# The opening of a gated-GLU and spectral kernel: weights on a second queue, pinned orders, and the left-over columns split after the transpose

## The chip, the cores and the metric

One core of a Trainium2 chip runs the whole program. The metric is device time in microseconds of one execution; three executions of the kernel before took 1441.42, 1441.58 and 1442.97 us (median 1441.58). A separate execution was profiled; its trace gives the rows below. Its span, from the first to the last instruction, is 1439.6 us.

The engines: TensorE (PE in the profile; PEld is its weight load), VectorE (DVE), ScalarE (ACT), GpSimd (POOL) and SyncE (SP), which here only issues transfers. ScalarE can issue transfers too, on a queue of its own.

## The reference

With S = 2048 rows, D = 576 columns, F = 4608 hidden columns, all in float32:

```python
xn = layernorm(x)                                   # over the 576 columns, eps 1e-5
X  = rfft2(xn) * (w_r + 1j * w_i)                   # over rows and columns
A  = irfft2(X, s=(2048, 576))
B  = (sigmoid(xn @ w_gate) * (xn @ w_up)) @ w_down
return x + A + B
```

## The kernel before

**Numbers.** A float32 matrix is split into a high part (rounded to fp32r, which TensorE takes at full rate) and a low part (the rest). A product is the sum of high x high, low x high and high x low.

**Rows.** The 2048 rows go in two halves ("pairs", p = 0 and 1) of eight tiles of 128 rows; a half is two chunks (c = 0, 1) of four tiles (m = 0 to 3), 512 rows each. The 576 columns of x are two blocks of 288 = 128 + 128 + 32. The 32 left-over columns get one matmul of 96 rows: high, high and low part stacked against high, low and high part of the weights. So a product of a 288-block with a 128-column weight block is seven matmuls of 128x512: four for the high and low combinations of `STEPS` on the 256 columns with high x, two with low x, one for the stacked left-over columns (index 2 in X and in w).

**Blocks of weights.** F is 36 blocks (f, or u = f + 36p) of 128 columns. `load_raw` brings a block's gate and up columns into `raw` (four quarters: B12, B22, B21, B11; two pieces per quarter, the second one copying the 32 left-over rows four times), eight transfers per block, two buffers. The first two blocks (`make_p`, f = 0, 1) use the four quarters as they are (`plain`: four products of a chunk); the later ones (`make_w`, `unit`) form sums of quarters for seven products in place of eight. `parts` rounds on ScalarE (L231) and makes the low parts on VectorE (L233, and L235 for 32 rows of the stacked piece). The result is stored to memory (`wsp`) for the second half, where `get_w` loads it instead.

**The transposed input.** X holds seven 288-blocks of the normalised rows, transposed, in fp32r: A11, A12 (chunk 0), A21, A22 (chunk 1), and the sums S1 to S4. `moments` and `scales` give mean and 1/std (VectorE, with a ScalarE square root in the opening, L360); `prep_hi` normalises a tile (ScalarE, L409). `fill(p, k, mm)` makes two tiles of one block: six transposes on TensorE into a PSUM pair (L438, L439), two copies on ScalarE (L442 high parts; L443 the left-over columns), one subtraction on VectorE (L444, low parts). The left-over columns are split before the transpose: `rem_hi` (ScalarE, L391) writes two copies of the high part, `rem_lo` (VectorE, L396) the low part, for two blocks at once, and TensorE transposes the 96 columns (L439). There are 16 fills in a half, four of them in the opening.

**Order.** A scheduler places instructions by program order and by when it takes their inputs to be ready; `placed` (through `keep_in_program_order`) pins one behind what stands before it on its engine, while `late_input` is set. Each engine and each queue then runs strictly in order.

**The opening.** L889: x tiles 0 to 3 on SP, raw block 0, tiles 4 and 5, raw block 1, tiles 6 and 7. TensorE multiplies by an identity meanwhile (L904, L922). Tiles 0 and 1 are normalised, then 2 and 3; A11 and A12 are filled for tiles 0, 1 and then 2, 3; block 0 is split (`mk`); the statistics of tiles 4 to 7 follow (L931). `plain` then runs (f, c) = (0,0), (1,0), (0,1), (1,1) in the banks A or B and E; beside it chunk 1 is prepared (`second_chunk`), then S1 to S4 (`factors`, `late`), and blocks 2 and 3 are made. From `unit` 2 on, the down products (`down`, `po`) run between the products, and VectorE adds them to `acc`.

**PSUM.** Two pairs of banks (tag pp) are shared by the fills, the down products and the later stages; single banks A, B, and two E.

Of the kernel before, what the change touches and what calls it, by code (L numbers as in the profile page):

```python
# [16 lines left out]
P = 128  # L17
# [115 lines left out]
def spectral_glu_kernel(ctx: ExitStack, tc: tile.TileContext, x, w_r, w_i, w_gate, w_up, w_down, out):  # L133
# [77 lines left out]
    def load_raw(f):  # L211
        cols = slice(f * P, (f + 1) * P)

        RAW[f] = raw = R["pool"].tile([P, 4, 3, P], F32, tag="raw", name=f"raw{f}", bufs=2)
        for src, blks in ((w_gate, (3, 2)), (w_up, (0, 1))):
            v = src.rearrange("(h r) f -> h r f", h=2)
            for h, b in enumerate(blks):
                nc.sync.dma_start(raw[:, b, :KT, :], v[h, :KT * P, cols].rearrange("(k p) f -> p k f", p=P))  # L218
                nc.sync.dma_start(raw[:, b, KT, :], v[h:h + 1, KT * P:, cols].to_broadcast([4, REM, P]))
# [8 lines left out]
    def parts(w, src, i, n):  # L228

        o = w[:, i:i + n]  # L230
        placed(nc.scalar.activation(o[:, :, :3, :], src, AF.Copy))  # L231
        yield
        placed(nc.vector.tensor_tensor(o[:, :, 3:, :], src[:, :, :KT, :], f32(o[:, :, :KT, :]), op=OP.subtract))  # L233
        r = slice(REM, 2 * REM)
        nc.vector.tensor_tensor(o[r, :, KT, :], src[r, :, KT, :], f32(o[r, :, KT, :]), op=OP.subtract)  # L235
        yield
# [28 lines left out]
    def make_p(f):  # L265
# [76 lines left out]
    def stats(srcs, t0, pool, table=False):  # L342

        for k, src in enumerate(srcs):
            moments(src, t0 + k, pool)
        scales(t0, len(srcs), pool, table)

# [6 lines left out]
    def scales(t0, n, pool, table):  # L354
# [3 lines left out]
        nc.vector.tensor_scalar(ve, mv[:, ts, 1], EPS, None, op0=OP.add)  # L358
        if table:
            nc.scalar.activation(w0, ve, AF.Sqrt)  # L360
            nc.vector.reciprocal(r0, w0)
            steps = 1
        else:

            nc.vector.tensor_scalar(w1.bitcast(I32), ve.bitcast(I32), 1, None, op0=OP.logical_shift_right)
            nc.vector.tensor_scalar(r0.bitcast(I32), w1.bitcast(I32), -1.0, float(0x5F3759DF), op0=OP.mult, op1=OP.add)
            steps = 3
        nc.vector.tensor_scalar(ve, ve, -0.5, None, op0=OP.mult)
# [14 lines left out]
    XS, XR, RM = {}, {}, {}  # L383
# [4 lines left out]
    def rem_hi(p, m, i, tag, bufs):  # L388
        rem = XS[m][:, i:i + 2, KT * P:]
        rm = R["pool"].tile([P, 2, 3, REM], F32R, tag=tag, name=f"{tag}{p}_{m}_{i}", bufs=bufs)  # L390
        nc.scalar.activation(rm[:, :, :2], rem.unsqueeze(2).to_broadcast([P, 2, 2, REM]), AF.Copy)  # L391
        RM[m, i] = rm

    def rem_lo(m, i):
        rm = RM[m, i]
        placed(nc.vector.tensor_tensor(rm[:, :, 2], XS[m][:, i:i + 2, KT * P:], f32(rm[:, :, 0]), op=OP.subtract))  # L396
        for k in range(2):
            XR[m, i + k] = rm[:, k].rearrange("p a b -> p (a b)")

    def rem_parts(p, m, i, tag, bufs):  # L400
        rem_hi(p, m, i, tag, bufs)
        rem_lo(m, i)

    def prep_hi(p, m, c):
# [5 lines left out]
        rem_hi(p, m, 2 * c, "rma", 2)  # L410

    def prep_lo(m, c):
        rem_lo(m, 2 * c)

    def prep(p, m, c):
        prep_hi(p, m, c)
        prep_lo(m, c)

    def sums(p, m):
# [5 lines left out]
        rem_parts(p, m, 3, "rma", 2)  # L425
        rem_parts(p, m, 1, "rm34", TPC)

    XP = {"A11": 0, "A12": 1, "A21": 2, "A22": 3, "S4": 1, "S3": 2, "S2": 3, "S1": 4}

    def fill(p, k, mm):  # L430

        i, j0 = XA[k], XP[k]
        cols = slice(2 * mm * P, (2 * mm + 2) * P)
        pt = pair(f"px{p}_{k}_{mm}")
        for j in range(2):
            m = 2 * mm + j
            for q in range(KT):
                nc.tensor.transpose(pt[:, 0, (2 * q + j) * P:(2 * q + j + 1) * P], XS[m][:, j0, q * P:(q + 1) * P], idf)  # L438
            nc.tensor.transpose(pt[:KR, 1, j * P:(j + 1) * P].bitcast(F32R), XR[m, j0], idr)  # L439
        v = pt[:, 0].rearrange("p (q s) -> p q s", q=KT)  # L440
        o = X[:, i, :, cols]
        nc.scalar.activation(o[:, :KT], v, AF.Copy)  # L442
        nc.scalar.activation(o[:KR, KT], pt[:KR, 1, :2 * P], AF.Copy)  # L443
        nc.vector.tensor_tensor(o[:, KT + 1:], v, f32(o[:, :KT]), op=OP.subtract)  # L444
# [201 lines left out]
    def prod(bank, w, x, start, stop, skip=False):  # L646
        for j, (sx, sw) in enumerate(STEPS):
            nc.tensor.matmul(bank, w[:, sw, :], X[:, x, sx, :], start=start and j == 0, stop=stop and j == len(STEPS) - 1,  # L648
# [11 lines left out]
    def plain(u, c, beside):  # L660
# [7 lines left out]
        for i, (b, k) in enumerate(((0, 1), (0, 2), (1, 1), (1, 2))):  # L668
            prod(bank[b], w[:, WP[f"B{k}{b + 1}"]], XA[f"A{c + 1}{k}"], k == 1, k == 2)
# [215 lines left out]
    nc.vector.memset(rstd[:, :1], 1.0)  # L885
    nc.scalar.dma_start(f32(idr), con["id"])
    nc.scalar.dma_start(idf, con["id"])
    nc.scalar.activation(nmr[:, :1], rstd[:, :1], AF.Sqrt)
# [14 lines left out]
    for n, (o, r) in enumerate(todo):  # L903
        nc.tensor.matmul(o, idr[r], eye[r], start=id(o) not in opened, stop=n + 2 >= len(todo), skip_group_check=True)  # L904
        opened.add(id(o))
    for m in range(TPC):
        new_xs(0, m)
    mk = make_p(0)
    for m in (0, 1):
        moments(acc[m], m, R["pool"])  # L910
    scales(0, 2, R["pool"], True)
    for m in (0, 1):
        prep_hi(0, m, 0)
    for m in (2, 3):
        moments(acc[m], m, R["pool"])
    for m in (0, 1):
        prep_lo(m, 0)
    scales(2, 2, R["pool"], True)
    for k in ("A11", "A12"):
        fill(0, k, 0)  # L920
# [225 lines left out]
```

## Time and profile before

| | |
|---|---|
| median of three runs | 1441.58 us (1441.42 to 1442.97) |
| the profiled execution | span 1439.6 us |
| TensorE matmul busy | 1425.9 us, 99% |
| VectorE busy | 1093.5 us, 76% |
| ScalarE busy | 652.3 us, 45% |
| GpSimd busy | 4.8 us |
| mean granted TensorE clock | 0.996 |

How the rows are read. A timeline row gives start (us from the span's start), time taken, engine, line, operation, out<-in tiles, shape and count; in brackets the idle time of that engine just before it and what ended it. A row of waits gives engine, tile and line, whom it waited for, then total us, times, longest. A row of a stretch gives its bounds and length, then busy us and number of instructions of PE, PEld, DVE, ACT and POOL, the granted TensorE clock (1.00 is full), the share of DMA time and GB/s. A row of a line or tile gives operation, tiles, count, shortest/median/longest ns, first and last start. A row of the chain gives start, length and what the end of the program was waiting for at that time. SPq and ACTq are transfers being issued.

### The profile page before, as it was taken

How to read it: one execution, taken by the hardware profiler on the slowest of the kernel's cores; microseconds unless marked ns; L12 is line 12 of the kernel's file. 1: busy time of each engine (PE TensorE's matmuls, PEld its weight loads, DVE VectorE, ACT ScalarE, POOL GpSimd, SP SyncE). 2: the span in 40 equal slices, each digit the busy share in tenths (PEclk: the TensorE clock that was granted, in tenths of full speed). 3: DMA queues.
4: the chain of work that ended last, by engine and by line, in shares of the span. 5: the costliest groups of instructions: out<-in, count | busy, mean ns of one | idle time of the engine just before them, and what ended most of it. 6: DMA issues, size and time to landing. Idle time of an engine off the chain costs nothing.

```text
span 1439.6 us, 21954 instructions
## 1 busy us (share of the span) xinstructions
PE 1425.9 (99%) x8073; PEld 1254.3 (87%) x8073; DVE 1093.5 (76%) x1798; ACT 652.3 (45%) x1122; POOL 4.8 (0%) x21
## 2 busy tenths in 40 slices
PE   8999999999999999999999999999999999999998
PEld 5888888888888888888888888888888889899997
DVE  6988788888888888756366787767888877766784
ACT  5644444444444444444345444444555534443432
POOL 0000000000000000000000000000000000000000
PEclk8999999999999999999999999999999999999999
DMA  6588788787777778664667767668998887776642
GB/s 209 207 277 294 263 295 285 254 274 258 263 261 255 262 254 277 230 231 167 226 210 203 212 197 214 196 198 275 271 275 272 267 276 246 228 224 198 204 126 83
DMA packets 184747, 338.86 MB, mean 235 GB/s; under 512 B 15808, under 2 KB 108480, under 8 KB 179776
## 3 DMA queue, kind: packets, MB, share of 16 engines
q1 hardware_dynamic: 183712, 336.15, 72.2%
q8 instruction: 64, 1.05, 0.3%
q10 hardware_dynamic: 928, 1.31, 0.3%
q14 instruction: 43, 0.35, 0.1%
HBM read 201.28 MB, written 136.12 MB: 234 GB/s over the span
## 4 chain that ended last, share of the span: by engine, by line
PE 94%; DVE 2%; DMA 1%; SPq 1%; ACT 1%; issue 1%; DVEq 0%; ACTq 0%
PE pB L648 23%; PE po L755 18%; PE pE L648 16%; PE pA L648 15%; PE ps L846 12%; PE pd L491 2%; PE pe L605 2%; PE pc L549 1%; PE py L576 1%; PE pa L503 1%; PE pb L532 1%; DMA raw<-in_B_w_up 1%; PE pf L475 1%; PE pz L588 1%; SPq L218 0%
## 5 line engine op out<-in xcount | busy, mean ns | idle before, releaser
L648 PE MATMUL pB<-X,w 128*128 128x512 f32 x1484 | 383.0, 395 | 1.9 <-ACT w L231 1.5
L648 PEld LDWEIGHTS pB<-X,w 128*128 128x128 f32 x1484 | 267.8, 188 | 51.8 <-ACT w L231 1.9
L648 PE MATMUL pE<-X,w 128*128 128x512 f32 x1064 | 272.5, 392 | 0.2 <-DVE y L713 0.2
L648 PE MATMUL pA<-X,w 128*128 128x512 f32 x1008 | 259.4, 395 | 0.3 <-DVE X L444 0.2
L648 PEld LDWEIGHTS pE<-X,w 128*128 128x128 f32 x1064 | 192.7, 188 | 34.6 <-DVE y L713 0.7
L648 PEld LDWEIGHTS pA<-X,w 128*128 128x128 f32 x1008 | 184.5, 190 | 33.9 <-DVE X L444 0.7
L755 PE MATMUL po<-wd,hh 128*128 128x288 f32 x1216 | 210.9, 295 | 0.0
L846 PE MATMUL ps<-wf,hs 128*128 128x288 f32 x1260 | 206.0, 296 | 0.3 <-issue 0.3
L846 PEld LDWEIGHTS ps<-wf,hs 128*128 128x128 f32 x1260 | 189.3, 188 | 19.4 <-DVE qs L856 1.9
L755 PEld LDWEIGHTS po<-wd,hh 128*128 128x128 f32 x1216 | 184.4, 188 | 11.2
L759 DVE TENSOR_TENSOR acc<-acc,po 128x576 f32<-128x576 f32 x168 | 126.0, 750 | 77.9 <-PE po L755 76.8
L231 ACT ACTIVATE w<-raw 128x768 fp32r<-128x768 f32 (+1 forms) x106 | 100.8, 952 | 115.6 <-PE pE L648 47.5
L755 PE MATMUL po<-wd,hl 128*128 128x288 f32 x608 | 128.9, 293 | 0.0
L856 DVE TENSOR_TENSOR qs<-qs,ps 128x576 f32<-128x576 f32 x112 | 84.1, 751 | 28.6 <-PE ps L846 27.9
L755 PEld LDWEIGHTS po<-wd,hl 128*128 128x128 f32 x608 | 98.7, 189 | 0.0
L733 DVE TENSOR_TENSOR y<-y,g 128x1024 f32<-128x1024 f32 x67 | 82.0, 1223 | 4.4 <-DVE y L732 0.5
L233 DVE TENSOR_TENSOR w<-raw,w 128x512 fp32r<-128x512 f32 (+1 forms) x106 | 82.0, 773 | 4.3 <-ACT w L231 3.3
L856 DVE TENSOR_TENSOR acc<-acc,ps 128x576 f32<-128x576 f32 x90 | 67.5, 750 | 22.9 <-PE ps L846 22.5
L716 ACT ACTIVATE g<-pB 128x512 f32<-128x512 f32 x68 | 40.7, 598 | 93.6 <-PE pB L648 93.5
L782 ACT ACTIVATE hs<-y 128x512 fp32r<-128x512 f32 x105 | 64.5, 628 | 34.3 <-DVE y L820 10.3
L732 DVE TENSOR_TENSOR y<-v,pE 128x512 f32<-128x512 f32 x67 | 45.9, 686 | 39.4 <-PE pE L648 39.3
L713 DVE TENSOR_TENSOR y<-v,pE 128x512 f32<-128x512 f32 x68 | 46.7, 687 | 33.7 <-ACT v L712 33.0
(166 smaller groups left out, 1678.8 us busy)
## 6 DMA issues: line engine op xcount, KB each, us to landing
w<-wsp SPq DMA_DIRECT2D x246, 320.0 KB
wsp<-w SPq DMA_DIRECT2D x34, 2240.0 KB
wdsp<-wd SPq DMA_DIRECT2D x36, 576.0 KB
wf<-tsp SPq DMA_DIRECT2D x60, 288.0 KB
wf<-wdsp SPq DMA_DIRECT2D x45, 288.0 KB
std<-in_B_w_down SPq DMA_DIRECT2D x36, 288.0 KB
raw<-in_B_w_gate SPq DMA_DIRECT2D x72, 128.0 KB
raw<-in_B_w_up SPq DMA_DIRECT2D x72, 128.0 KB
```

What stands on the lines that cost most here:

```text
L231: placed(nc.scalar.activation(o[:, :, :3, :], src, AF.Copy))
L233: placed(nc.vector.tensor_tensor(o[:, :, 3:, :], src[:, :, :KT, :], f32(o[:, :, :KT, :]), op=OP.subtract))
L648: nc.tensor.matmul(bank, w[:, sw, :], X[:, x, sx, :], start=start and j == 0, stop=stop and j == len(STEPS) - 1, skip_group_check=skip)
L713: nc.vector.tensor_tensor(y[:, 1], v[:, 1], bank["E"], op=OP.add)
L716: nc.scalar.activation(g[:, 1], bank["B"], AF.Sigmoid)
L732: nc.vector.tensor_tensor(y[:, 0], v[:, 0], bank["E"], op=OP.add)
L733: nc.vector.tensor_tensor(y, y, g, op=OP.mult)
L755: nc.tensor.matmul(pd[:, b, :HD], h[i], w[k][b], start=g == 0 and n == 0, stop=g == G - 1 and n == 2)
L759: nc.vector.tensor_tensor(a, a, pd[:, :, :HD], op=OP.add)
L782: nc.scalar.activation(hs[:, 0], src, AF.Copy)
L846: nc.tensor.matmul(pd[:, i, :HD], h[:, a, m], w[:, b], start=q == 0, stop=q == 2)
L856: nc.vector.tensor_tensor(o, o, pd[:, :, :HD], op=OP.add)
```

## The change

- Block 0's raw weights are issued on ScalarE's queue; block 1's on SP directly behind x tiles 0 to 3; x tiles 4 to 7 behind them.
- Half of block 0's split (quarters 2 and 3) goes from ScalarE and VectorE to GpSimd.
- The square root takes its eps as a bias, so that one addition no longer stands ahead of it.
- `rem_hi` and `rem_lo` go. A fill (`lift`) transposes the 32 left-over columns in float32, copies them twice on ScalarE (32 x 256 each) and subtracts on VectorE (32 x 256), all behind the transposes. This holds for all fills of the kernel.
- In the opening the parts of the four fills are written out in an order by hand and pinned; A12's transposes use the E and B banks.
- The first two products run their matmuls with low parts of x last (`LOW_LAST`).
- The stores of blocks 0 and 1 (`keep_p`) are issued later, behind the raw loads of blocks 2 and 3.

```diff
+                put = (eng or nc.sync).dma_start
+                put(raw[:, b, :KT, :], v[h, :KT * P, cols].rearrange("(k p) f -> p k f", p=P))
+                put(raw[:, b, KT, :], v[h:h + 1, KT * P:, cols].to_broadcast([4, REM, P]))
...
-    def parts(w, src, i, n):
+    def parts(w, src, i, n, idle=False):
         o = w[:, i:i + n]
-        placed(nc.scalar.activation(o[:, :, :3, :], src, AF.Copy))
-        yield
-        placed(nc.vector.tensor_tensor(o[:, :, 3:, :], src[:, :, :KT, :], f32(o[:, :, :KT, :]), op=OP.subtract))
+        if idle:
+            nc.gpsimd.tensor_copy(o[:, :, :3, :], src)
+        else:
+            placed(nc.scalar.activation(o[:, :, :3, :], src, AF.Copy))
+        yield
+        eng = nc.gpsimd if idle else nc.vector
+        placed(eng.tensor_tensor(o[:, :, 3:, :], src[:, :, :KT, :], f32(o[:, :, :KT, :]), op=OP.subtract))
         r = slice(REM, 2 * REM)
-        nc.vector.tensor_tensor(o[r, :, KT, :], src[r, :, KT, :], f32(o[r, :, KT, :]), op=OP.subtract)
+        placed(eng.tensor_tensor(o[r, :, KT, :], src[r, :, KT, :], f32(o[r, :, KT, :]), op=OP.subtract))
...
-            yield from parts(w, raw[:, i:i + 2], i, 2)
-        nc.sync.dma_start(wsp[f][:, :4 * 5 * P], f32(w[:, :4]).rearrange("p a k m -> p (a k m)"))
-        yield
+            yield from parts(w, raw[:, i:i + 2], i, 2, f == 0 and i == 2)
+    def keep_p(f):
+        nc.sync.dma_start(wsp[f][:, :4 * 5 * P], f32(WS[f][:, :4]).rearrange("p a k m -> p (a k m)"))
...
-        nc.vector.tensor_scalar(ve, mv[:, ts, 1], EPS, None, op0=OP.add)
         if table:
-            nc.scalar.activation(w0, ve, AF.Sqrt)
-            nc.vector.reciprocal(r0, w0)
+            nc.scalar.activation(w1, mv[:, ts, 1], AF.Sqrt, bias=nmr[:, NT - 1:])
+            nc.vector.tensor_scalar(ve, mv[:, ts, 1], EPS, -0.5, op0=OP.add, op1=OP.mult)
+            nc.vector.reciprocal(r0, w1)
...
+    def lift(k, mm, main, rest):
+        for j in range(2):
+            src = XS[2 * mm + j][:, XP[k]]
+            for q in range(KT):
+                nc.tensor.transpose(main[:, (2 * q + j) * P:(2 * q + j + 1) * P], src[:, q * P:(q + 1) * P], idf)
+            nc.tensor.transpose(rest[:REM, j * P:(j + 1) * P], src[:, KT * P:], idf)
+        v, r = main.rearrange("p (q s) -> p q s", q=KT), rest[:REM, :2 * P]
+        o = X[:, XA[k], :, 2 * mm * P:(2 * mm + 2) * P]
+        def rems():
+            placed(nc.scalar.activation(o[:REM, KT], r, AF.Copy))
+            return nc.scalar.activation(o[REM:2 * REM, KT], r, AF.Copy)
+        return (lambda: nc.scalar.activation(o[:, :KT], v, AF.Copy),
+                rems,
+                lambda: nc.vector.tensor_tensor(o[:, KT + 1:], v, f32(o[:, :KT]), op=OP.subtract),
+                lambda: nc.vector.tensor_tensor(o[2 * REM:KR, KT], r, f32(o[:REM, KT]), op=OP.subtract))
+
     def fill(p, k, mm):
...
+        for part in lift(k, mm, pt[:, 0], pt[:, 1]):
+            part()
...
+    LOW_LAST = ((0, 0), (1, 1), (0, 3), (1, 4), (3, 0), (4, 1), (2, 2))
...
+            prod(bank[b], w[:, WP[f"B{k}{b + 1}"]], XA[f"A{c + 1}{k}"], k == 1, k == 2, steps=STEPS if u + c or b else LOW_LAST)
...
-    for i in range(TPP):
+    for i in range(TPC):
         new_acc(0, i)
-        if i in (TPC - 1, TPC + 1):
-            load_raw(i // TPC)
+    load_raw(0, nc.scalar)
+    load_raw(1)
+    for i in range(TPC, TPP):
+        new_acc(0, i)
...
     mk = make_p(0)
+    next(mk)
...
+    p1, p2 = pair("px0_A11_0"), [ps.tile([P, CW], F32, tag="bE", name=f"px0_A12_0{i}", bufs=2) for i in range(2)]
+    hi1, rem1, lo1, low1 = lift("A11", 0, p1[:, 0], p1[:, 1])
+    hi2, rem2, lo2, low2 = lift("A12", 0, *p2)
+    placed(hi1())
+    placed(rem1())
+    identity(4)
     for m in (2, 3):
         prep(0, m, 0)
+    placed(lo1())
+    p3, p4 = pair("px0_A11_1"), ps.tile([P, CW], F32, tag="bB", name="px0_A12_1")
+    hi3, rem3, lo3, low3 = lift("A11", 1, p3[:, 0], p3[:, 1])
+    hi4, rem4, lo4, low4 = lift("A12", 1, p4, p2[1][:, 2 * P:])
+    for part in (hi3, lo3, low1, hi2, rem3, low3, hi4, lo2, lo4, rem2, rem4, low2, low4):
+        placed(part())
     for _ in mk:
         pass
-    stats([acc[TPC + m] for m in range(TPC)], TPC, R["pool"], table=True)
+    for m in range(TPC):
+        moments(acc[TPC + m], TPC + m, R["pool"])
+    scales(TPC, TPC, R["pool"], True)
...
                 load_raw(2)
+                keep_p(0)
             if p == 0 and n == 1:
                 load_raw(3)
+                keep_p(1)
```

More of the change, by code (lines that the diff above doesn't have):

```diff
@@ L340, in load_x @@
             (eng or nc.sync).dma_start(dst[i * N1:(i + 1) * N1, :D], r)
[L342 to L346, printed above, removed]
     def moments(src, t, pool):
@@ L905, in spectral_glu_kernel, with identity @@
         opened.add(id(o))
+    def identity(n):
+        for _ in range(n):
+            tc.keep_in_program_order(nc.tensor.matmul(b0, idr, eye, start=False, stop=True, skip_group_check=True))
     for m in range(TPC):
```

67 lines of the change are left out of this document (11 added, 56 removed).

## The prediction

> **What bounds the kernel now.** I read the page's head first, then TensorE's waits over the whole run, then busy time by stretch, then the order of instructions up to 92 us.
>
> ```profile
> span 1439.6 us, 21954 instructions
> PE 1425.9 (99%) x8073; PEld 1254.3 (87%) x8073; DVE 1093.5 (76%) x1798; ACT 652.3 (45%) x1122; POOL 4.8 (0%) x21
> PE pB L648 <- ACT w L231: 1.5, 1, 1.5
> PE px_S L438 <- DVE X L444: 0.5, 1, 0.5
> PE pE L648 <- DVE y L713: 0.2, 1, 0.2
> 46.00:66.00 20.00, 19.52 (x110) 16.16 (x109) 19.07 (x34) 16.28 (x32) 0.00 (x0) 1.00 0.53 203
> 66.00:91.00 25.00, 24.78 (x147) 22.07 (x145) 19.54 (x30) 9.34 (x13) 0.00 (x0) 1.00 0.76 257
> ```
>
> TensorE is the bound nearly everywhere: it lacks 13.7 us of work in the span, and most of that lies in the opening. But one stretch is shared: from 46 to 66 us VectorE works 19.07 of 20.00 us. So whatever the opening wins must pass through a stretch where VectorE has almost nothing to spare. The clock is the second thing:
>
> ```profile
> 14.50:15.00 0.50, 0.19 (x2) 0.19 (x3) 0.42 (x2) 0.50 (x2) 0.00 (x0) 0.86 0.79 216
> 21.50:22.00 0.50, 0.50 (x4) 0.41 (x3) 0.00 (x0) 0.00 (x0) 0.00 (x0) 0.81 1.19 354
> 28.50:29.00 0.50, 0.50 (x3) 0.41 (x2) 0.03 (x1) 0.49 (x2) 0.00 (x0) 0.52 0.77 211
> 31.50:32.00 0.50, 0.50 (x3) 0.46 (x2) 0.50 (x4) 0.50 (x3) 0.00 (x0) 0.57 0.36 135
> ```
>
> The granted clock (the column after POOL) falls to half at about 14.9, returns at 21.7, falls again at 28.5 and returns at 31.9. The second fall follows the 1.5 us wait for w; the waits of 0.5 and 0.2 us cost no clock.
>
> **The change part by part.** The end of the opening is the start of block 1's first product (bank pB). Who sets it:
>
> ```profile
> 18.02 2.44 SPq L340 DMA_DIRECT2D acc<-in_A_x  x4
> 7.16 0.20 ACT L360 ACTIVATE rs<-rs 128x2 f32<-128x2 f32 x1 [4.07 <-DVE rs L358]
> 16.38 0.79 PE L648 MATMUL pA<-X,w 128*128 128x512 f32 x1
> 18.83 0.41 DVE L235 TENSOR_TENSOR w<-raw,w 32x256 fp32r<-32x256 f32 x1
> 19.28 0.82 DVE L351 BATCH_NORM_STATS2 st<-acc 128x6 f32<-128x288 f32 x2
> 23.96 0.90 DVE L351 BATCH_NORM_STATS2 st<-acc 128x6 f32<-128x288 f32 x2 [2.68 <-DMA acc<-in_A_x]
> 26.07 0.17 DVE L358 TENSOR_SCALAR rs<-mv 128x4 f32<-128x4 f32 x1
> 26.27 0.20 ACT L360 ACTIVATE rs<-rs 128x4 f32<-128x4 f32 x1 [8.20 <-DVE rs L358]
> 26.42 0.84 ACT L231 ACTIVATE w<-raw 128x768 fp32r<-128x768 f32 x1
> 27.31 3.01 PE L648 MATMUL pB<-X,w 128*128 128x512 f32 x7 [1.50 <-ACT w L231]
> L218 SPq DMA_DIRECT2D raw<-in_B_w_gate x8: 378/584/1553, 5.8 to 34.7; - x8
> ```
>
> pB waits for ScalarE's rounding of w1 (26.42), which is behind the square root (26.27), which is behind the statistics of tiles 4 to 7; tile 6 is 2.68 us late because its rows are issued only at 18.02, after sixteen weight pieces.
>
> *Weights 0 on ScalarE's queue.* SP then issues x 0 to 3, weights 1 (8 pieces at 0.58 = 4.6 us, 5.8 to 10.4) and x 4 to 7 (8 at 0.6, to about 15.3). Before, the last x issue ended at 20.46 and VectorE stopped waiting at 23.96, 3.5 us later; now that is about 19, and tile 6 is wanted at 21.3. The 2.68 us go. The 8 issues on ScalarE take 4.6 us from 3.1 (the engine was idle for 4.07 us before the square root at 7.16), to 7.7; the root is late by the difference less the 0.17 us addition ahead of it that goes, some 0.4 (bounds 0, if pieces cost the 0.38 of the row's minimum, to 2.0, if they cost twice the median beside SP's). 0.4 is taken, and it rides down the whole chain.
>
> *Orders pinned, A12 in idle banks, low parts last.* The four copies of A12 no longer stand between tiles 0, 1 and tiles 2, 3 on ScalarE, which prepares the latter about a microsecond sooner and no longer splits block 0's gate half (0.84 a split) among them, so the first product, at 16.38 now, can start near 14.8. That is not the end of the opening: VectorE still has, after the last A11 copy (about 14.8), three 128x512 low parts at 0.69, four new 32x256 ones at 0.42 and block 0's pair of 0.69 and 0.42 (rows below): 4.8 us, done at about 19.6 where before it was 19.24. The half of block 0's split that leaves for GpSimd is what pays for the four new ones. The sums of tiles 4 to 7 (1.0 each by 19.28 to 21.28) then end at 23.6; the root follows at 23.7, w1 0.15 behind it (26.27 to 26.42) and pB 0.89 behind that, at 24.8 instead of 27.31: **the opening gives 2.5 us.** TensorE's first two products lie inside that; starting earlier only lengthens its wait for w1, except that the first half-clock stretch then lies mostly under the wait. GpSimd's part is priced by
>
> ```profile
> 0.73 3.08 POOL L893 MEMSET X<- 32x3584 f32 x1 [0.29 <-POOLq L1135]
> L233 DVE TENSOR_TENSOR w<-raw,w x4: 686/692/693, 15.5 to 29.9; 128x512 fp32r<-128x512 f32 x4
> L235 DVE TENSOR_TENSOR w<-raw,w x4: 415/416/416, 16.2 to 30.7; 32x256 fp32r<-32x256 f32 x4
> ```
>
> 0.86 ns an element makes 1536 elements 1.3 us; three times that would be 4. The weights land near 9 (an estimate: the fourth issue ends at 5.4, and 3.5 us to land as above) and the low parts are wanted by the third matmul at 15.7, so it is hidden from either price.
>
> SBUF — State Buffer (the Trainium skill), section "SBUF: two separate sides", speaks against this part: GpSimd and a VectorE instruction with two SBUF inputs lock each other out for a whole instruction. No run here shows it yet; it would hold the small scale instructions of tiles 2 and 3 at about 11 us by up to one GpSimd instruction, 1.3 us by that page's rule and the row's price, and the sum would end 1.3 us later.
>
> *Left-over columns split late* concerns all 32 fills, 28 of them behind the opening. What they cost now:
>
> ```profile
> L439 PEld LDWEIGHTS px_S<-idr,rma x16: 124/125/127, 43.4 to 693.3; 128*96 128x96 f32 x16
> L438 PEld LDWEIGHTS px_S<-idf,xa x64: 137/141/146, 43.1 to 705.2; 128*128 128x128 f32 x64
> 43.33 0.38 PE L438 MATMUL px_S<-idf,xa 128*128 128x128 f32 x2
> 43.88 0.45 PE L648 MATMUL pE<-X,w 128*128 128x512 f32 x1
> 31.85 0.35 DVE L396 TENSOR_TENSOR rma<-xa,rma 128x64 fp32r<-128x64 f32 x2
> 46.79 0.37 ACT L443 ACTIVATE X<-px_S 96x256 fp32r<-96x256 f32 x1
> 47.19 0.69 DVE L444 TENSOR_TENSOR X<-px_S,X 128x512 fp32r<-128x512 f32 x1 [0.41 <-ACT X L443]
> 47.80 0.75 DVE L292 TENSOR_TENSOR wd<-std,wd 128x576 fp32r<-128x576 f32 x1
> 48.82 0.96 DVE L233 TENSOR_TENSOR w<-raw,w 128x768 fp32r<-128x768 f32 x1 [0.28 <-ACT w L231]
> ```
>
> TensorE: the six transposes of a fill (two tiles by three) take 0.55 (43.33 to 43.88). The third becomes an f32 one of 32 columns. Loading 96 columns takes 16 ns less than 128, so 32 take 48 less; it may cost half as much again as its share of the 0.55 (+0.09 a fill) or half of it (-0.09). Between these ends I take nought, by the nearest row, the load of 96 columns: 2.5 us either way over 28 fills are the bounds. ScalarE: one copy more of 256 columns (0.37, the L443 row) against one short split fewer; even, and it has room (16.28 of 20.00). VectorE: per fill one 32x256 subtraction more (0.42, the L235 row) against one short one less (two take 0.35). Over 16 fills of the second half of the rows that is hidden:
>
> ```profile
> 640.00:710.00 70.00, 70.00 (x423) 61.58 (x422) 36.74 (x72) 32.15 (x71) 0.13 (x2) 1.00 0.60 200
> ```
>
> VectorE has 33 us free there. In the first half it is not: eight fills lie between 43 and 64 us. The first two subtractions find the idle 0.41 and 0.28 us before 47.19 and 48.82 and expose 0.15; ScalarE's second copy ahead of the second fill's low part adds 0.37; six more at 0.42 add 2.5; the four short ones that stand there go, -0.7. **Together +2.3 us on VectorE** by 68.5 us. Why that counts:
>
> ```profile
> SPq L293 <- DVE wd L292: 14.5, 5, 8.1
> 68.54 0.33 SPq L293
> 76.51 5.18 DMA raw<-in_B_w_up
> 90.28 0.70 DVE y L713
> 91.03 1.88 PE pE L648 x7
> ```
>
> SP's store of the down weights waits for VectorE, block 4's weights are issued behind it, land at 81.7, are split, and TensorE's last product of block 3 waits at 91 for y, queued on VectorE behind that split. This chain moves with VectorE, not with TensorE. It starts 2.5 earlier and is 2.3 longer: at 91 us TensorE is where it was, less 0.2, with a longer wait there.
>
> *Stores of w0 and w1 later on SP*, 1.3 MB each (four blocks of 128x640 f32), behind the pieces of blocks 2 and 3. Block 3's pieces can go once w1 is split (30.7 less 2.5), 4.6 us; the store of w1 takes 6 at the 203 GB/s of 46 to 66 us; behind it stand the first down weights, there by 41 and used before 47.8. Hidden; 2 us late at half that rate. *LOW_LAST* reorders seven matmuls, no price. *Square root with bias*: counted.
>
> **Sum** against the profile's span: 1439.6 - 2.5 + 2.3 = 1439.4; the median of the runs shown is 2.0 above that span, so **1441.4 us**.
>
> **The rivals.** *Faster: the gain passes.* If y of block 3 is queued ahead of the last parts of the split, or the new subtractions fall into VectorE's gaps, TensorE keeps 2.5 and drops the 0.5 and 0.2 us waits: 1441.6 - 3.2 = 1438.4, and with the transposes halfway to their cheap end (28 x 0.045 = 1.3) 1437.1; I give it 1437.7. For it: 5.5 us of idle VectorE at 66 to 91 us, and TensorE's waits there are only 0.2 us now. Against it: that idle time lies behind the late weights, where it can't be used.
>
> *Slower: the clock falls at 91 us.* TensorE arrives up to 2 us early at the wait for y. If that wait grows past what it bore without loss (0.5) to the 1.5 us that halved the clock at 28.5, unit 4 starts at half speed for 3.4 us (28.5 to 31.9; loss 1.7) up to 6.8 us (14.9 to 21.7; loss 3.4), behind a bound that had not moved. With the dear transposes of the second half (16 x 0.09 = 1.4) it is 1441.4 + 1.7 + 1.4 = 1444.5, up to 1446; I give it 1444.9. It decides from a wait of about 1 us on. TensorE: Matmul & The Clock Gate (the Trainium skill), section "Part 1: The HAM clock gate", puts a low window at about 3.4 us; the trace agrees (28.5 to 31.9). For it: VectorE's extra work. Against it: shorter waits spread before it (bank releases at 57 to 61 us) would eat the lead.
>
> *It does not do what it says* (ScalarE's issues as dear as 1.2 us, tiles 4 to 7 no earlier) is inside the bounds: 2.0 later, 1443.4.
>
> **How the numbers follow.** Forecast 0.43, its own range 1439.2 to 1443.6; faster rival 0.35; slower rival 0.22. With 0.2% (2.9 us), about what a measurement of this kernel can tell from no change, the borders are 1438.7 and 1444.5: faster 0.35 (most of the rival, a little of the forecast's edge), slower 0.21, the same 0.44. The range that leaves out no more than 2 in 10 is 1436.6 to 1445.3: from a microsecond under the faster rival to a little over the slower.
>
> **What would show it.** Right: pB starts near 24.8 and tile 6's wait is gone; the first product near 14.8; VectorE without gaps from 47 to 69; block 4's split and TensorE's wait at 91 where they were, that wait over 1 us; the six transposes of a fill still 0.55 us. Wrong: no wait at 91 (the faster rival), half clock after it (the slower), VectorE instructions held near 11 us while GpSimd works, or a fill's transposes at 0.64 us.

## The result, and the profile after

| | before | after |
|---|---|---|
| median of five runs each, same chip | 1441.42 us | 1449.08 us (1448.44 to 1450.12) |
| ratio, 95% interval | | 1.0054, 1.0042 to 1.0066 |
| span of the profiled execution | 1439.6 us | 1447.3 us |

The change made the kernel 7.7 us slower; a tie at 1441.4 us was forecast. The head of the page after, then four rows of TensorE's waits over the run (whom it waited for; total us, times, longest):

```profile
span 1447.3 us, 21975 instructions
PE 1426.8 (99%) x8073; PEld 1252.9 (87%) x8073; DVE 1102.7 (76%) x1793; ACT 658.4 (45%) x1121; POOL 7.6 (1%) x24
```

```profile
PE px_A L409 <- ACT xa L393: 4.5, 2, 3.1
PE pB L632 <- ACT w L235: 2.5, 1, 2.5
PE pE L632 <- DVE X L420: 1.4, 1, 1.4
PE px_S L409 <- DVE X L421: 0.4, 2, 0.2
```

TensorE's busy time is 0.9 us more; the rest of the 7.7 us is time in which it waits or runs short of work. The first wait is new in size: the transposes of the opening wait for normalised tiles (`xa`). The third is new: a product waits for the low part of a fill (L420). The fourth, a fill's transposes waiting for the end of an earlier fill, stood before too (0.5 us, once); its last step is now L421, the low part of the left-over columns. The forecast's wait for y near 91 us is not among them.

The opening after, by start time (a bracket gives the engine's idle time before the instruction and what ended it):

```profile
0.73 8.84 SPq L346 DMA_DIRECT2D acc<-in_A_x  x8
8.81 0.55 ACTq L220 DMA_DIRECT2D raw<-in_B_w_up  x1
15.31 6.00 SPq L346 DMA_DIRECT2D acc<-in_A_x  x8
...
8.18 0.82 DVE L351 BATCH_NORM_STATS2 st<-acc 128x6 f32<-128x288 f32 x2 [2.39 <-DMA raw<-in_B_w_up]
9.42 0.30 ACT L359 ACTIVATE rs<-mv,nmr 128x2 f32<-128x2 f32 x1 [6.30 <-DMA raw<-in_B_w_gate]
10.30 0.82 POOL L233 CAST w<-raw 128x768 fp32r<-128x768 f32 x1 [6.49 <-DMA raw<-in_B_w_gate]
10.34 0.80 DVE L373 SCALAR_TENSOR_TENSOR rstd<-rs 128x2 f32<-128x2 f32 x1
14.40 0.82 DVE L351 BATCH_NORM_STATS2 st<-acc 128x6 f32<-128x288 f32 x2 [2.08 <-DMA acc<-in_A_x]
19.95 1.63 PE L632 MATMUL pA<-X,w 128*128 128x512 f32 x6 [0.45 <-ACT X L418]
25.43 0.82 DVE L351 BATCH_NORM_STATS2 st<-acc 128x6 f32<-128x288 f32 x2
29.39 0.30 ACT L359 ACTIVATE rs<-mv,nmr 128x4 f32<-128x4 f32 x1 [5.16 <-DVE mv L352]
30.47 0.79 PE L632 MATMUL pB<-X,w 128*128 128x512 f32 x1 [2.47 <-ACT w L235]
```

and the rows of the kernel before that answer to its first and its statistics rows, tiles 1 and 3 of x:

```profile
0.73 5.06 SPq L340 DMA_DIRECT2D acc<-in_A_x  x8
5.86 0.82 DVE L351 BATCH_NORM_STATS2 st<-acc 128x6 f32<-128x288 f32 x2
9.24 0.77 DVE L351 BATCH_NORM_STATS2 st<-acc 128x6 f32<-128x288 f32 x2
```

The eight issues of x tiles 0 to 3 on SP, which the change does not touch, take 8.84 us in place of 5.06. Tile 1's statistics start at 8.18 in place of 5.86, tile 3's at 14.40 in place of 9.24, both at the end of an idle time. (The releaser printed for tile 1 is a weight transfer; the instruction itself reads only `acc`, so this is the event nearest in time and not its input.) The rest follows, 3 to 4 us late: the preparation of tiles 2 and 3 at 16.94 (12.67 before), the first product at 19.95 (16.38 before), the square root for tiles 4 to 7 at 29.39 (26.27 before), pB at 30.47 (27.31 before). Tiles 4 to 7 cost no wait any more: 25.43 has none, where tile 6 had cost 2.68 us before. But their rows are not issued sooner: the last issue ends at 21.31, 20.46 before. VectorE comes to them 6 us later (25.43, 19.28 before), and that is why it finds them there.

The share of DMA time and the rate from 2 to 8 us (the last two columns), and what each queue moved in these 6 us (packets, MB, share of DMA time; by the issues, q1 carries SP's transfers and q10 ScalarE's), before and then after:

```profile
2.00:8.00 6.00, 5.48 (x14) 3.97 (x16) 2.76 (x12) 1.28 (x3) 1.81 (x1) 1.00 0.82 232
q1 hardware_dynamic: 918, 1.31, 77.2%
```

```profile
2.00:8.00 6.00, 5.23 (x17) 3.71 (x18) 1.03 (x3) 1.10 (x2) 1.81 (x1) 1.00 0.95 225
q1 hardware_dynamic: 451, 0.83, 56.7%
q10 hardware_dynamic: 1083, 0.52, 38.6%
```

Before, these 6 us at 232 GB/s carry nearly x alone (1.31 MB); after, x (0.83 MB) and block 0's weights (0.52 MB) share 225 GB/s. What x lacks, the weights got, and the DMA engines were busier (0.95 of the time, 0.82 before) for slightly fewer bytes. The Trainium skill, DMA: Bandwidth & Descriptors, section "Issuing engines are not separate DMA queues", says that queues of different engines are served by the same 16 DMA engines, so that spreading transfers over them gains no bandwidth; the two rates agree.

**Where the delay grows.** The start of one and the same product in the two traces (after minus before, at the time of before): +3.6 us at the first product, +3.2 at pB (27.31), +3.65 at unit 2 (53.72), +5.2 at 63.49 and at 91.03, +5.0 from 161 to 640, +7.3 behind the fills of the second half (932), +7.05 at the last product (1422), and 0.65 more behind it. So there are three places: the opening, a stretch near 60 us, and the second half's fills.

Near 60 us, after:

```profile
54.52 0.38 PE L409 MATMUL px_S<-idf,xa 128*128 128x128 f32 x2
55.10 1.86 PE L632 MATMUL pE<-X,w 128*128 128x512 f32 x7
60.87 0.74 PE L632 MATMUL pE<-X,w 128*128 128x512 f32 x2 [1.41 <-DVE X L420]
...
55.38 0.60 ACT L418 ACTIVATE X<-px_S 128x512 fp32r<-128x512 f32 x1 [1.46 <-PE px_S L410]
56.92 0.35 ACT L415 ACTIVATE X<-px_S 32x256 fp32r<-32x256 f32 x1
58.22 0.38 ACT L416 ACTIVATE X<-px_S 32x256 fp32r<-32x256 f32 x1
59.68 0.41 DVE L240 TENSOR_TENSOR w<-raw,w 32x256 fp32r<-32x256 f32 x1
60.12 0.69 DVE L420 TENSOR_TENSOR X<-px_S,X 128x512 fp32r<-128x512 f32 x1
```

The six transposes take 0.58 us (54.52 to 55.10; 0.55 before). Their 256 columns are rounded at once (55.38). The two left-over copies come only at 56.92 and 58.22, as ScalarE rounds weights between, and the low part, which stands behind them in program order, starts at 60.12, behind a weight split on VectorE. TensorE stands for 1.41 us on it. Busy time by stretch, after:

```profile
46.00:66.00 20.00, 18.35 (x99) 14.52 (x98) 18.15 (x32) 15.18 (x30) 0.00 (x0) 1.00 0.35 145
640.00:710.00 70.00, 69.80 (x412) 60.72 (x411) 40.03 (x69) 32.87 (x64) 0.14 (x2) 1.00 0.57 191
```

From 46 to 66 us TensorE lost work (18.35 of 20, 19.52 before). In the second half VectorE still has 30 us free, and TensorE is delayed all the same. One fill's drain there (the copies and subtractions that empty its two PSUM banks), before and then after:

```profile
705.08 0.60 ACT L442 ACTIVATE X<-px_S 128x512 fp32r<-128x512 f32 x1 [1.16 <-PE px_S L439]
705.58 0.37 ACT L443 ACTIVATE X<-px_S 96x256 fp32r<-96x256 f32 x1
705.98 1.45 DVE L444 TENSOR_TENSOR X<-px_S,X 128x512 fp32r<-128x512 f32 x2 [1.34 <-ACT X L443]
```

```profile
709.95 0.60 ACT L418 ACTIVATE X<-px_S 128x512 fp32r<-128x512 f32 x1
710.44 0.36 ACT L415 ACTIVATE X<-px_S 32x256 fp32r<-32x256 f32 x1
710.81 0.37 ACT L416 ACTIVATE X<-px_S 32x256 fp32r<-32x256 f32 x1
711.21 0.69 DVE L420 TENSOR_TENSOR X<-px_S,X 128x512 fp32r<-128x512 f32 x1
711.92 0.42 DVE L421 TENSOR_TENSOR X<-px_S,X 32x256 fp32r<-32x256 f32 x1
...
655.90 0.76 PE L739 MATMUL po<-wd,hh 128*128 128x288 f32 x4 [0.18 <-DVE X L421]
712.48 0.41 PE L409 MATMUL px_S<-idf,xa 128*128 128x128 f32 x2 [0.18 <-DVE X L421]
```

Before, the two banks of a fill are free about 1.6 us after the first copy starts (705.08 to about 706.7, the first of the two subtractions of the last row). After, it is 2.4 us (709.95 to 712.34), and what needs the banks next waits for the new last step, L421. That is so at three places of the second half: at 655.90 and 712.48 (last two rows) and at 711.22. There the distance from the start of the matmul before is 0.57, 0.66 and 0.47 us, where matmuls of a product follow each other at 0.23; together that is 1.0 us.

### The profile page after: what moved, and what is told of

Read it like the earlier page. It is cut to its first block, busy times and chain, and to the rows that moved or that the text cites. A ratio compares the mean times of both kernels' runs of the same rounds, so it can differ in the third digit from the quotient of the medians.

```text
span 1447.3 us, 21975 instructions
## 1 busy us (share of the span) xinstructions
PE 1426.8 (99%) x8073; PEld 1252.9 (87%) x8073; DVE 1102.7 (76%) x1793; ACT 658.4 (45%) x1121; POOL 7.6 (1%) x24
## 4 chain that ended last, share of the span: by engine, by line
PE 94%; DVE 2%; ACT 1%; DMA 1%; issue 1%; SPq 0%; ACTq 0%; DVEq 0%
PE pB L632 23%; PE po L739 18%; PE pE L632 16%; PE pA L632 15%; PE ps L830 12%; PE pd L473 2%; PE pe L587 2%; PE pc L531 1%; PE py L558 1%; PE pa L485 1%; PE pb L514 1%; PE pf L457 1%; DMA raw<-in_B_w_up 1%; PE pz L570 0%; DVE X L420 0%
## 5 line engine op out<-in xcount | busy, mean ns | idle before, releaser
L716 DVE TENSOR_TENSOR y<-v,pE 128x512 f32<-128x512 f32 x67 | 46.0, 686 | 40.6 <-PE pE L632 40.5
```

Source lines behind the costliest of these rows:

```text
L716: nc.vector.tensor_tensor(y[:, 0], v[:, 0], bank["E"], op=OP.add)
```

## The experiments

All times are medians beside runs of the kernel before on the same chip (1441.44, 1441.43, 1441.59 and 1441.30 us in the four groups); ratios have 95% intervals. The table gives the start of the same product, minus its start in the kernel before, in us; the heads are times of the kernel before.

| kernel | first product 16.4 | pB 27.3 | unit 2 53.7 | 63.5 | 91.0 | 375 | 932 | last 1422 | median |
|---|---|---|---|---|---|---|---|---|---|
| after | 3.6 | 3.2 | 3.7 | 5.2 | 5.2 | 5.0 | 7.3 | 7.1 | 1449.08 |
| e1_raw0_sp | -0.2 | 0.8 | -0.1 | 1.5 | 1.4 | 1.2 | 3.5 | 3.4 | 1444.38 |
| e4_before_raw0_act | 5.3 | 3.5 | 2.3 | 2.4 | 2.4 | 2.4 | 2.5 | 2.4 | 1444.27 |
| e8_tiny_act | -0.2 | 1.0 | 0.7 | 0.7 | 0.7 | 0.7 | 0.8 | 0.9 | 1442.67 |
| e10_half_act | 2.1 | 1.2 | 0.1 | 0.1 | 0.1 | 0.1 | 0.2 | 0.0 | 1441.43 |
| e3_early_cols | 4.2 | 3.8 | 4.4 | 4.4 | 4.0 | 3.9 | 3.9 | 3.8 | 1445.61 |
| e5_before_late_cols | -0.2 | 0.3 | 0.8 | 2.4 | 2.4 | 2.2 | 4.4 | 4.2 | 1445.55 |
| e11_lo_first | -0.1 | 0.0 | 0.3 | 1.8 | 1.6 | 1.5 | 5.1 | 4.9 | 1446.24 |
| e12_long_drain | -0.1 | 0.0 | 3.9 | 3.7 | 4.8 | 4.7 | 6.5 | 6.6 | 1447.12 |
| e2_no_gpsimd | 2.9 | 5.3 | 4.3 | 5.9 | 5.9 | 5.7 | 7.9 | 7.8 | 1450.48 |
| e7_both | -1.5 | -0.4 | -1.0 | -1.0 | -1.4 | -1.5 | -1.5 | -1.6 | 1440.46 |
| e6_before_x_first | -0.2 | -2.9 | -3.0 | -2.4 | -2.4 | -2.3 | -2.3 | -2.3 | 1439.36 |
| e9_x_first_gpsimd | -0.1 | -2.1 | -3.1 | -2.4 | -2.8 | -3.0 | -2.9 | -3.1 | 1438.92 |

### Block 0's weights on the second queue

**e1_raw0_sp**: the changed kernel, block 0's weights back on SP behind x tiles 0 to 3.

```diff
-    load_raw(0, nc.scalar)
+    load_raw(0)
```

> The changed kernel, with block 0's weights back on SP behind x tiles 0 to 3. Theory 1 (block 0's pieces on the second queue move beside x tiles 1 to 3 and hold them up): x is issued by 5.8 us again, the statistics of tiles 2 and 3 are no longer late (14.4 becomes about 9.5), block 1's first product moves from 30.5 to about 26.5, and the time falls by 3 to 5 us to 1444 to 1446. Theory 2 (GpSimd holding VectorE is what delays the opening): the time stays within 1 us of 1449.1. Theory 3 (the opening costs little, the late split of the left-over columns costs nearly all): likewise within 1 us.

1444.38 us, ratio 1.0024 (1.0014 to 1.0033): 4.7 us of the 7.7 come back. A row of the timeline and one of TensorE's waits:

```profile
9.34 0.77 DVE L351 BATCH_NORM_STATS2 st<-acc 128x6 f32<-128x288 f32 x2
```

```profile
PE pE L632 <- ACT w L235: 3.6, 1, 3.6
```

Tile 3 is on time again (9.34; 9.24 before), the eight issues take 5.06 us, and the first product starts at 16.17. The delay is gone at unit 2, the later two losses stay. pB is at 28.15, better than 30.47 but not at the 26.5 of the expectation. What limits the opening now is the up half of block 0, which the pinned order puts behind the left-over copies.

**e4_before_raw0_act**: the reverse, the kernel before with that one edit.

```diff
...
-            load_raw(i // TPC)
+            load_raw(i // TPC, nc.scalar if i == TPC - 1 else None)
```

> The kernel before, with block 0's weights alone moved to ScalarE's queue. Theory 1: x tiles 1 to 3 land late as in the changed kernel, block 1's first product moves from 27.3 to 29 to 31 us, and as VectorE's chain to 91 us moves with the opening, the time rises by 2 to 4 us to 1443.4 to 1445.4. If the queue alone is harmless, tiles 4 to 7 come earlier and the time falls by up to 2 us, to 1439.4.

1444.27 us, 1.0019 (1.0009 to 1.0028), 2.8 us slower. Tile 3 in its timeline:

```profile
14.65 0.82 DVE L352 BATCH_NORM_STATS2 st<-acc 128x6 f32<-128x288 f32 x2 [3.20 <-DMA acc<-in_A_x]
```

The same late x rows in a kernel without the rest of the change. The first product is 5.3 us late, 2.4 stay.

**e8_tiny_act** tells issuing from transferring: the kernel before, with eight transfers of 512 bytes each on ScalarE's queue into a scratch tile.

```diff
+        if i == TPC - 1:
+            dum = fix.tile([8, P], F32, name="dum")
+            for n in range(8):
+                nc.scalar.dma_start(dum[n:n + 1], w_gate[n:n + 1, :P])
         if i in (TPC - 1, TPC + 1):
             load_raw(i // TPC)
```

> The kernel before, with eight more DMAs on ScalarE's queue where the change issues block 0's eight pieces, each of one row of 512 bytes into a scratch tile that nobody reads. It tells issuing from transferring. Theory 1 (the 512-byte packets of block 0's weights take the transfer time of the x rows): no delay, the eight x issues on SP take about 5.06 us and the statistics of tile 3 stand at 9.24 us as before, 1441.4 us. Rival (two queues that issue at once slow each other, whatever they move): the eight x issues take near 8.8 us, tile 3's statistics stand at 13 to 14.7 us, 1444 us, as where block 0's weights alone went to that queue (1444.27).

```profile
0.73 6.35 SPq L340 DMA_DIRECT2D acc<-in_A_x  x8
```

```profile
9.43 0.82 DVE L351 BATCH_NORM_STATS2 st<-acc 128x6 f32<-128x288 f32 x2 [0.18 <-DMA acc<-in_A_x]
```

1442.67 us, 1.0010 (1.0001 to 1.0020): halfway between the two expectations. Issuing on a second queue does lengthen SP's issues, by 1.3 us over eight, and delays with SP all that it issues later (pB 1.0 us late). But tile 3, the point of the question, is only 0.2 us late. Of the 5.2 us of the changed kernel the rest comes from what the transfers carry.

**e10_half_act**: the kernel before, with only the gate half (4 of the 8 pieces) on ScalarE's queue.

```diff
...
+                put = (eng if eng and src is w_gate else nc.sync).dma_start
...
```

> The kernel before, with only the gate half of block 0's weights (4 of the 8 pieces, 128 blocks of 512 bytes a piece and chunk) on ScalarE's queue and the up half on SP's. It asks whether the delay of the x rows goes with the bytes on the second queue. None, only eight tiny transfers: tile 3's statistics at 9.43 us; all eight pieces: 14.65 us. Theory 1 (shared transfer time, in proportion to the bytes): in the middle, tile 3's statistics at 11.5 to 12.5 us, first product 2 to 3 us later than before, 1442 to 1443.5 us. Rival (a second queue with large transfers costs the same whatever it carries): 14 us or more and 1444 us.

```profile
11.79 0.77 DVE L352 BATCH_NORM_STATS2 st<-acc 128x6 f32<-128x288 f32 x2
```

Tile 3 at 11.79 and the first product 2.1 us late, as expected of a cost in proportion to the bytes: nothing (the eight tiny transfers), half and all of the block give 9.43, 11.79 and 14.65. (Half the bytes are half the packets too; which of the two counts is not told apart.) The time missed its expectation of 1442 to 1443.5: 1441.43 us, 0.9999 (0.9990 to 1.0008). The delay is 1.2 us at pB and gone at unit 2. Here the trace shows no half clock after pB, where the kernel before is at half clock from 28.5 to 31.9 us; that this is what made the delay good was not tested, and e6, which has no half clock there either, gains only 0.1 us from pB to unit 2.

### The left-over columns

**e3_early_cols**: the changed kernel with the old order (split, then transpose) in the 28 fills behind the opening.

```diff
...
-        for part in lift(k, mm, pt[:, 0], pt[:, 1]):
-            part()
...
+            nc.tensor.transpose(pt[:KR, 1, j * P:(j + 1) * P].bitcast(F32R), XR[m, j0], idr)
...
```

> The changed kernel, with the left-over columns split ahead of the transpose again in the 28 fills behind the opening. Theory 3 (late split: +2.0 us between 30 and 91 us, +2.0 between 640 and 712 us): 3.5 to 4.5 us less, 1444.6 to 1445.6, with block 1's first product where it is (30.5). If VectorE's work in 46 to 66 us is not what TensorE waited for at 91 us, only the second half's 2.0 come back, 1447.

1445.61 us, 1.0028 (1.0017 to 1.0038): 3.5 us back. The opening keeps its delay (3.8 at pB), and from there on the delay no longer grows: 3.8 at the last product.

**e5_before_late_cols**: the kernel before with the late split in those 28 fills alone.

```diff
...
+        if p or k not in ("A11", "A12"):
+            return fill2(p, k, mm)
...
```

> The kernel before, with the left-over columns split late in the 28 fills behind the opening and nothing else of the change. Theory 1 (a third transpose of 32 f32 columns costs what one of 128 does, some 0.1 us a fill, and VectorE's added subtractions hold up TensorE in the first half): 1.3 to 1.6 us later by the last product of block 3 (91.03 us before), 2.0 us more over the 16 fills of the second half, 1445.0 us. Theory 2 (the loss in the first half comes only from meeting the late opening of the changed kernel): nothing at 91 us, 2.0 us in the second half, 1443.4 us. As predicted (transposes at nought, VectorE's 2.3 us borne by the wait at 91 us): 2 us later at 91 us, nothing in the second half, 1443.4 us too, so the place tells these two apart.

1445.55 us, 1.0029 (1.0018 to 1.0040), 4.1 us slower: 0.5 us between pB and unit 2, 1.6 us between unit 2 and 63.5, and 2.2 us in the second half's fills. The places are those of theory 1, with more than its 1.3 to 1.6 us ahead of 91 us, but its reason for the second half was not right: the transposes of a fill in the second half take 0.57 to 0.60 us, 0.56 before. Over the stretch that holds all 16 fills (the same 214 products), which grew from 90.86 to 93.03 us, the 96 transposes account for 0.46 us more and the products for 1.62: up to 0.03 each (0.4 in all) for those directly behind a fill, 1.0 at three places where TensorE waits for the last subtraction of a drain, as in the changed kernel, and the rest not traced. So TensorE's own work is 0.9 of the 2.2 us, more than nothing, and the wait for drains about as much.

**e11_lo_first**: as e5, with VectorE's subtraction of the 256 columns ahead of ScalarE's left-over copies in program order.

```diff
...
-        for part in lift(k, mm, pt[:, 0], pt[:, 1]):
+        hi, rems, lo, low = lift(k, mm, pt[:, 0], pt[:, 1])
+        for part in (hi, lo, rems, low):
             part()
```

> As the kernel with the late left-over columns alone (1445.55 us), but in those 28 fills VectorE's subtraction of the 256 columns stands ahead of ScalarE's two copies of the left-over columns, so that it runs beside them. There the fill's transposes are only 0.02 to 0.04 us longer than before, while a fill's two PSUM banks are held for two copies more in a row: 0.60 + 0.36 + 0.37 on ScalarE, then 0.69 + 0.42 on VectorE, 2.4 us, against 0.60 + 0.37, then 0.69, 1.7 us before. Theory 1 (the next fill waits for the banks, and the low parts come later): the drain is 1.7 us again; the 1.4 us wait for a low part near 58 us goes or is under 0.8, the second half loses 0.5 us or less where it lost 1.9, 1443 us or less. Rival (the transposes and the change of operand kind on TensorE itself): the second half still loses 1.9 us, 1444.5 to 1445.5 us.

```profile
PE px_S L435 <- DVE X L447: 1.5, 2, 0.8
PE po L782 <- DVE X L447: 1.5, 1, 1.5
```

1446.24 us, 1.0035 (1.0022 to 1.0048): a miss for both. The second half lost 3.6 us (375 to 932), more than either expected; the loss near 60 us stayed (1.5 us). The scheduler now puts two fills' large copies on ScalarE ahead of both pairs of left-over copies, so L447, which frees the banks, comes later still, and TensorE waits for it by name: 0.83 and 0.70 us near 58 and 64 us, 1.46 us at 653.64. That TensorE waits for the end of the drain is thus seen in the rows; this order was no remedy.

**e12_long_drain**: the kernel before with its own transposes, and a drain lengthened by repeating a copy and a small subtraction in the same 28 fills.

```diff
+        if p or k not in ("A11", "A12"):
+            nc.scalar.activation(o[:KR, KT], pt[:KR, 1, :2 * P], AF.Copy)
         nc.vector.tensor_tensor(o[:, KT + 1:], v, f32(o[:, :KT]), op=OP.subtract)
+        if p or k not in ("A11", "A12"):
+            nc.vector.tensor_tensor(o[:REM, KT + 1], v[:REM, 0], f32(o[:REM, 0]), op=OP.subtract)
```

> The kernel before, its transposes unchanged; in the 28 fills behind the opening ScalarE makes the copy of the left-over columns twice and VectorE repeats the subtraction of 32 rows, so that the fill's banks are held some 0.8 us longer. It doubles part of the work and changes no value. Theory 1 (the length of the drain is what costs): 1.2 to 2 us lost in the second half's fills, and 1.5 to 3 us up to 91 us, where VectorE carries 12 subtractions more and ScalarE 12 copies more: 1444.5 to 1446 us. Rival (the transposes): nothing in the second half, 1441.4 to 1443.5 us.

```profile
655.99 1.66 PE L652 MATMUL pB<-X,w 128*128 128x512 f32 x6 [0.69 <-ACT v L716]
```

1447.12 us, 1.0040 (1.0026 to 1.0054). Between 375 and 932 us it loses 1.8 us with unchanged transposes, where the late columns lose 2.2 and the rival expected nothing. But what is waited for is not the same: the longest wait named there is a product's, 0.69 us at 655.99, for ScalarE's copy of another product out of its bank (L716), which queues behind the fills' copies. So longer drains alone can cost as much, by a queue on ScalarE; that the changed kernel's 1.8 us come this way is not shown. Before 91 us it loses more than expected, 4.8 us, with the same kind of wait (1.52 us at 40.87, 1.38 at 61.04); there it carries the old splits as well, so that part does not price the change.

### The rest of the opening

**e2_no_gpsimd**: the changed kernel with block 0's gate half split on ScalarE and VectorE.

```diff
-            yield from parts(w, raw[:, i:i + 2], i, 2, f == 0 and i == 2)
+            yield from parts(w, raw[:, i:i + 2], i, 2)
```

> The changed kernel, with block 0's gate half split on ScalarE and VectorE again. Theory 2 (GpSimd holds VectorE): the 0.80 us instruction at 10.3 us becomes 0.16, and the time falls by 1 us or more. Theory 1 (the transfers): GpSimd cost 0.6 us there, the same work on ScalarE and VectorE costs 0.8 to 1.1 us later; the time is the same within 1 us, or up to 1.5 us longer.

1450.48 us, 1.0064 (1.0049 to 1.0079): not faster than the change but, by the medians, 1.4 us slower (0.8 by the last product in the table; the intervals overlap). The instruction that took 0.80 us takes 0.16 again, so GpSimd did hold it (last section), but taking GpSimd's work away gives nothing back: the hold is not what made the kernel slower.

**e7_both**: the changed kernel with e1's and e3's edits together.

> The changed kernel with both suspects undone: block 0's weights behind x 0 to 3 on SP's queue, and the left-over columns split ahead of the transposes in the 28 fills behind the opening. What stays of the change: pinned order, A12 in idle banks, low parts last, the split on GpSimd, late stores of w0 and w1. Theory 1 (the two losses are separate and add): 1449.1 - 4.7 - 3.5 = 1440.9 us, level with before. Rival (the pinned order or the GpSimd split is a third loss that either of the two hides): 1443 us or more, with the delay present at the first product or at pB already.

1440.46 us, 0.9994 (0.9984 to 1.0003). The two losses are separate and add: 4.7 and 3.5 us taken alone, 8.6 together. What is left of the change is about 1 us of gain, not distinguishable from none. The first product starts at 14.92, but pB only at 26.93: a wait of 3.6 us for the up half of block 0, as in e1, and x tile 4, which VectorE waits 1.46 us for, now issued behind sixteen weight pieces.

**e6_before_x_first**: the kernel before, with x tiles 6 and 7 issued ahead of block 1's weights, and nothing else.

```diff
-        if i in (TPC - 1, TPC + 1):
-            load_raw(i // TPC)
+    load_raw(0)
+    for i in range(TPC, TPP):
+        new_acc(0, i)
+    load_raw(1)
```

> The kernel before, with x tiles 6 and 7 issued ahead of block 1's weights instead of behind them. Theory A (the step of the prediction: VectorE's wait of 2.68 us for tile 6 goes and the start of pB moves with it): pB at 24.8 us instead of 27.31, and if the lead passes the stretch from 46 to 66 us, 1438.9 us. Theory B (VectorE has nothing to spare at 46 to 66 us, so the lead is lost there): pB at 24.8, but unit 3's last product at 91 us as before, 1441.4 us. Theory C (block 1's weights, 2.4 us later, become the wait): pB at 27 to 28, 1441.4 to 1442.5 us.

```profile
21.06 0.85 DVE L351 BATCH_NORM_STATS2 st<-acc 128x6 f32<-128x288 f32 x2
23.47 0.84 ACT L231 ACTIVATE w<-raw 128x768 fp32r<-128x768 f32 x1
24.37 3.87 PE L648 MATMUL pB<-X,w 128*128 128x512 f32 x14 [0.43 <-ACT w L231]
```

1439.36 us (1439.26 to 1439.72), 0.9986 (0.9977 to 0.9996). Tile 6's wait is gone, pB starts at 24.37, and 2.3 us of the lead are kept to the last product: the stretch from 46 to 66 us does not swallow it. The order is another than the change's, which puts block 1's weights ahead of all four tiles 4 to 7.

**e9_x_first_gpsimd**: e6 and the GpSimd split of block 0's gate half.

```diff
+    load_raw(1)
...
+            yield from parts(w, raw[:, i:i + 2], i, 2, f == 0 and i == 2)
```

> The kernel before, with x tiles 6 and 7 ahead of block 1's weights (1439.36 us alone, pB at 24.37) and with the gate half of block 0's weights split on GpSimd, as the change has it. Theory 1 (the split is off the path on GpSimd, and ScalarE and VectorE gain 0.84 and 1.1 us ahead of the first product): first product at 15.4 to 15.8 us instead of 16.21, pB at 23.5 to 24.0, 1438.5 us. Rival (GpSimd and VectorE lock each other out: the short low parts of tiles 2 and 3 near 14.7 us and the scale instructions near 12 us are held by up to 1.3 us): first product no earlier than 16.2, 1439.4 us or up to 1 us more.

```profile
12.00 0.68 DVE L378 SCALAR_TENSOR_TENSOR nmr<-mv,rstd 128x2 f32<-128x2 f32 x1
16.30 0.47 PE L652 MATMUL pA<-X,w 128*128 128x512 f32 x1 [0.43 <-ACT X L446]
```

1438.92 us, 0.9985 (0.9976 to 0.9994): faster than both kernels, as e6 is, and not told apart from it. The first product came no earlier (16.30; 16.21 in e6), as the rival said, with a VectorE instruction held for 0.5 us, and pB came at 25.24 and not at 23.5 to 24.0; the time lies between the two expectations.

## Why the prediction was wrong, step by step

- **"Weights 0 on ScalarE's queue" is the step that failed.** It priced the issues on ScalarE (a square root 0.4 us late, at most 2.0) and took x tiles 0 to 3 on SP as untouched, so that what the weights' transfers take from x stood at nothing. The first root came 2.3 us late (9.42, 7.16 before), not for the issues but because tile 1's sums were done only at 9.25. e8 and e10 show that what is transferred beside x is what counts: tile 3's statistics came 5.2 us later, the first product 3.6 us later, and pB at 30.47 in place of the forecast 24.8. "The opening gives 2.5 us" became a loss of 3.2; that difference of 5.7 us is most of the miss. The sum's issues of x 4 to 7 "to about 15.3" fell with it: they ended at 21.31.
- **The lead through tiles 4 to 7**: that pB moves when tile 6's wait goes is right. e6 has pB at 24.37 (forecast 24.8) for that reason, with an order that the change does not have, and its lead passes the full stretch of VectorE, which was the faster rival's claim and not the forecast's. The profiled execution of e6 shows no half clock at all from 12 to 34 us, but the gain does not hang on it: executions of e6 with a mean clock of 0.997 took 1439.36 to 1439.72 us, those with 0.999 or 1.000 1439.26 to 1439.52.
- **The pinned order** does give a first product at 14.9 us (forecast 14.8), seen in e7, where x is on time. Its price, the up half of block 0 behind the left-over copies (a wait of 3.6 us in e1 and e7), was not in the sum; with x on time and both blocks' weights ahead of tiles 4 to 7, pB is at 26.93 (e7), not at 24.8.
- **GpSimd's split**: forecast as hidden, with 1.3 to 4 us of work; it took 2.8, and the changed kernel is no faster without it.
- **Transposes of the left-over columns at nought**: right within the bounds (0.09 us a fill either way), 0.57 to 0.60 us a fill for 0.56 and 0.03 more for the product behind it. It is not nought: 0.9 us over the 16 fills of the second half (e5).
- **"Over 16 fills of the second half that is hidden"** failed. VectorE has its 30 us free, and yet 2.3 us are lost there. e3 and e5 show that the late split is the cause. Of e5's 2.2 us, 0.5 are the transposes and 0.4 the products directly behind them; 1.0 is waiting for the end of drains that are 0.8 us longer, which is a length and does not show in VectorE's busy time; the rest is open. This step should have looked at who waits for the end of a drain, not at VectorE's idle time.
- **VectorE's 2.3 us before 68.5** had about the right size (2.1 us between pB and 91 us, 0.5 of them ahead of unit 2, where the sum counted nothing) and the wrong path. TensorE does not wait at 91 us; it waits 1.41 us at 60.87, for a low part that stands on VectorE behind a weight split. So the gain of the opening and this cost would never have met in one wait: e6 and e5 move the end each by its own amount.
- The slower rival, half clock after a wait at 91 us, did not occur: the granted clock is 1.00 from 33.4 us to the last product, and there is no such wait.

By place: 3.2 us to pB, 2.0 to 91 us, 1.8 from there to the last product, 0.65 behind it. The last was not followed up.

## What to carry to other kernels

A transfer that is moved to an idle queue is not free where the transfers it now runs beside are the ones waited for: count the bytes in flight ahead of the first use, and put loads in order of need on one queue before spreading them. The cost of more small steps behind a transpose is to be read also from the time for which its banks are held, and from who queues behind them, however idle the engine is. What paid here was no part of the change: x tiles 6 and 7 issued ahead of block 1's weights, on the one queue, gained 2.1 us alone (e6).

## What the runs showed of the hardware

- Two queues that carry large transfers share the rate, and the queue that started first has no precedence: 232 GB/s before and 225 after from 2 to 8 us, of which x got 1.31 and then 0.83 MB, with tile 3 of x 5.2 us later. In proportion to what the other queue carries: 9.43, 11.79 and 14.65 us with none, half and all of a block's eight pieces on the other queue.
- Even tiny transfers issued on ScalarE's queue lengthen SP's issues, from 0.63 to 0.79 us each (5.06 and 6.35 over eight).
- GpSimd holds up VectorE instructions with two SBUF inputs: the one at 10.34 took 0.80 us in place of 0.16 and ended at 11.14, just behind GpSimd's copy (10.30 to 11.12). The Trainium skill, SBUF — State Buffer, section "SBUF: two separate sides", says that the pair of ports is locked for the whole instruction of whichever came first; the trace agrees, and the price is one short hold of 0.6 us (0.5 in e9); without the split the changed kernel was not faster (e2).
